# A linear-attention layer: 640 output columns as 512 and 128 on one stationary block, keys one block ahead of values, and the last query norms first

## The chip, the cores and the metric

The kernel runs on one core of a Trainium2 chip. The metric is the device time of one execution in microseconds (us). Engines are named as in the profile: PE (TensorE, with PEld for its weight loads), DVE (VectorE), ACT (ScalarE), POOL (GpSimd) and SP (SyncE, here a queue that issues DMAs).

## The reference, cut to what matters

Four layers run one after the other on 2048 tokens of 640 features: A, B, A, B. Layer A is a recurrent attention with memory in 64 segments and takes most of the time. The change lies in layer B, a linear attention with 32 heads of 20 features:

```
qkv   = layernorm(x) @ wqkv                      # 2048 x 1920
pq,pk = q @ w_phi, k @ w_phi                     # per head, 20 x 20
phi_q = [softmax(pq), softmax(-pq)]              # and phi_k likewise
kv    = sum over tokens of phi_k^T v             # per head, 40 x 20
z     = sum over tokens of phi_k
o     = (phi_q @ kv) / (phi_q . z + 1e-6)
x     = x + o @ wo                               # wo is 640 x 640
```

## The kernel before

Layer B works on 16 blocks of 128 tokens, four blocks to a group, and has two stages with all of `kv` between them.

**First stage, groups 0 to 3.** For each group the rows are normalised and turned with TensorE transposes into `xnT`. `keys_values` (L403) then goes block by block. The keys' 640 columns are two products of 320 columns (`ps_pk`, L410, five matmuls each, one for each 128 input features); ACT takes exp(+) and exp(-) of each half (L413); DVE sums them by head (`sk`, L416) and takes reciprocals (`rk`, L418), which POOL copies into `vr` (L421). The values are again two products of 320 columns (`ps_v`, L425), which DVE scales by `rk` into `vr` (L429). Last come 14 small matmuls that add the block into `kv` (L435); they stay in three PSUM banks over all blocks. After the four blocks, `query_norms` (L451) runs for the group before: two sums over features (`ps_sq`, L457, six matmuls each), a logarithm of each on ACT (L349), exponentials (L342, L343) and DVE steps (L460, L344), and then, for each of the six head groups, one matmul `ps_e` (L465) and a DVE product (L466). Then `queries` (L440) makes six products of 512 columns (`ps_pq`, L446), whose exponentials ACT writes into `phi` (L449).

**Second stage, groups 0 to 3.** `denominators` (L523) is twelve matmuls `ps_den` (L527) with a stationary block of 64 columns, and then L349, L342, L343 and L344. `attention` (L531) makes, for each of six head groups, two matmuls `ps_num` (L538) and one `ps_e` (L541); ACT copies `ps_e` (L543) and DVE multiplies (L544). `output_rows` (L547) makes, for each of four blocks, two products of 320 columns with `wo` (`ps_wo`, L555), six matmuls each, of which five have 120 rows and the last has 40; DVE adds the residual (L557) and POOL issues the store (L559). In the first layer B the rows are also normalised for the layer A after it: DVE statistics (L222), two small POOL casts, ACT (L236, L237), the subtraction on POOL (L244), the scaling on ACT (L248), and a second store from POOL (L563).

Before the first stage, `multiply` (L1192) makes rows that layer A left over, as products of 512 and 128 columns on one stationary block (L1198 into `kv` banks, L1199 into `ps_post`), four times in a layer.

**PSUM.** There are eight banks: three for `kv`, two in the pool `pt` (`side_bank`, for `ps_post`, `ps_sq`, `ps_den` and both `ps_e`), and three in the pool `ps` (`bank`, for all the rest). A buffer that is taken again waits until the last reader of its former tile is done. A scheduler sets the order of layer B's instructions on each engine when the program is built; each engine then runs its instructions in that order.

Of the kernel before, what the change touches and what calls it, by code (L numbers as in the profile page):

```python
# [8 lines left out]
P = 128  # L9
BF16 = mybir.dt.bfloat16  # L10
F32 = mybir.dt.float32
ACT = mybir.ActivationFunctionType
ALU = mybir.AluOpType
# [18 lines left out]
def bcast_last(ap2, n):  # L32
    d = [list(x) for x in ap2.ap]
    assert len(d) == 2, d
    return ap3(ap2, [d[0], d[1], [0, n]])
# [80 lines left out]
class Kernel:  # L116
# [133 lines left out]
    def layer_B(self, x_dram, at_dram, xout_dram, xnext_dram, li, bp, post):  # L250


        nc, tc, KC, D = self.nc, self.tc, self.KC, self.Dm
        DH, H = self.DhB, self.HB
        HC = 6
        CH = DH * HC
        NC_ = -(-H // HC)
        sizes = [min(CH, D - CH * c) for c in range(NC_)]
        NG, NB = self.NG, self.NB
        HB2 = H // 2  # L260
        W2 = D // 2
        at = 0

        def take(nbytes):
# [5 lines left out]
        wo = self.view(take(NC_ * D * 2), NC_ * D * 2).rearrange("p (c m) -> p c m", m=D)  # L270
# [15 lines left out]
        wqkv = self.view(take(6 * D * KC), 6 * D * KC).rearrange("p (k n) -> p k n", k=KC)  # L286
# [3 lines left out]
        x2 = self.view(take(NB * D * 2), NB * D * 2).rearrange("p (b d) -> p b d", d=D)  # L290
# [2 lines left out]
        assert at <= ARENA - fb  # L293
        phi = self.view(ARENA - fb, fb).rearrange("p (s c t) -> p s c t", s=2, c=NC_)
        with tc.tile_pool(name=f"B{li}_kv", bufs=1, space=bass.MemoryType.PSUM, reuse_waits="tile") as kvp, \
                tc.tile_pool(name=f"B{li}_pt", bufs=2, space=bass.MemoryType.PSUM, reuse_waits="tile") as ptp, \
                tc.tile_pool(name=f"B{li}_ps", bufs=3, space=bass.MemoryType.PSUM, reuse_waits="tile") as pp:
            def bank(name="ps_b", dt=F32):
                return pp.tile([P, 512 if dt == F32 else 1024], dt, name=name, tag="bank")

            def side_bank(name):
                return ptp.tile([P, 512], F32, name=name, tag="side")

            nc.gpsimd.memset(wbd[:], 0.0)
            for i in range(HC):
                n = len(range(i, H, HC))
                nc.gpsimd.dma_start(out=wbd[DH * i:DH * i + DH, 0:n, DH * i:DH * i + DH],
                                    in_=self.B_w_phi[i:H:HC].rearrange("h d f -> d h f"))
# [73 lines left out]
            def fuse(j):  # L382
# [17 lines left out]
                        self.ev.copy(out=wqkv[:, k, D * j + CH * c0:D * j + CH * c0 + n], in_=ps[:, 0:n])  # L400
                nc.gpsimd.dma_start(out=self.fused_d[:, :, D * j:D * j + D], in_=wqkv[:, :, D * j:D * j + D])

            def keys_values(g, xnT):  # L403
                for b in range(4 * g, 4 * g + 4):
                    q = P * (b - 4 * g)
                    ek = eks.next().rearrange("p (s d) -> p s d", s=2)
                    for u in range(2):
                        ps = bank("ps_pk")
                        for k in range(KC):
                            nc.tensor.matmul(ps[:, 0:W2], lhsT=xnT[:, k, q:q + P],  # L410
                                             rhs=wqkv[:, k, D + W2 * u:D + W2 * u + W2], start=(k == 0), stop=(k == KC - 1))
                        for sg in range(2):
                            nc.scalar.activation(out=ek[:, sg, W2 * u:W2 * u + W2], in_=ps[:, 0:W2], func=ACT.Exp,  # L413
                                                 scale=1.0 - 2.0 * sg)
                    sk = bp.tile([P, 2 * H], F32, name="sk", tag="sk")
                    nc.vector.reduce_sum(out=sk[:], in_=ek[:, :, :].rearrange("p s (h f) -> p (s h) f", f=DH), axis=AX.X)  # L416
                    rk = bp.tile([P, 2, H], F32, name="rk", tag="rk")
                    nc.vector.reciprocal(out=rk[:, :, :].rearrange("p s h -> p (s h)"), in_=sk[:])  # L418

                    vr = vrs.next().rearrange("p (s h f) -> p s h f", s=2, h=H)  # L420
                    nc.gpsimd.tensor_copy(out=vr[:, :, :, DH], in_=rk[:])  # L421
                    for u in range(2):
                        ps = bank("ps_v")
                        for k in range(KC):
                            nc.tensor.matmul(ps[:, 0:W2], lhsT=xnT[:, k, q:q + P],  # L425
                                             rhs=wqkv[:, k, 2 * D + W2 * u:2 * D + W2 * u + W2], start=(k == 0),
                                             stop=(k == KC - 1))
                        for sg in range(2):
                            nc.vector.tensor_tensor(out=vr[:, sg, HB2 * u:HB2 * u + HB2, 0:DH],  # L429
                                                    in0=ps[:, 0:W2].rearrange("p (h f) -> p h f", f=DH),  # L430
                                                    in1=bcast_last(rk[:, sg, HB2 * u:HB2 * u + HB2], DH), op=ALU.mult)
                    for sg in range(2):
                        for c in range(NC_):
                            nh = sizes[c] // DH
                            nc.tensor.matmul(kv_out(sg, c), lhsT=ek[:, sg, CH * c:CH * c + sizes[c]],  # L435
                                             rhs=vr[:, sg, HC * c:HC * c + nh, :].rearrange("p h f -> p (h f)"),
                                             start=(b == 0 and (NC_ * sg + c) % 4 == 0), stop=(b == NB - 1),
                                             skip_group_check=True)

            def queries(g, xnT):  # L440
                tk = slice(512 * g, 512 * g + 512)
# [50 lines left out]
            waiting = None  # L492
            for g in range(NG):
                if g == 0:
                    xnT = first_xnT
                elif g == 1:
                    with tc.issue_after(turned.ins):
                        xnT = norm_T(g)
                else:
                    xnT = norm_T(g)  # L500
# [21 lines left out]
            def denominators(g):  # L522
                tk = slice(512 * g, 512 * g + 512)  # L523
                ps = side_bank("ps_den")
                for i in range(2 * NC_):
                    sg, c = i // NC_, i % NC_
                    nc.tensor.matmul(ps[0:64, :], lhsT=zm[0:sizes[c], sg, c, :], rhs=phi[0:sizes[c], sg, c, tk],  # L527
                                     start=(i == 0), stop=(i == 2 * NC_ - 1))
                return split_exp(log_rows(ps), -1.0)

            def attention(g, hl):  # L531
                tk = slice(512 * g, 512 * g + 512)
                oT = oTs.next().rearrange("p (c t) -> p c t", c=NC_)
                for c in range(NC_):
                    mc = sizes[c]
                    pn = bank("ps_num")
                    for sg in range(2):
                        nc.tensor.matmul(pn[0:mc, :], lhsT=kvm[0:mc, sg, c, 0:mc], rhs=phi[0:mc, sg, c, tk], start=(sg == 0),  # L538
                                         stop=(sg == 1))
                    pe = side_bank("ps_e")  # L540
                    nc.tensor.matmul(pe[0:mc, :], lhsT=expc[0:64, c, 0:mc], rhs=hl, start=True, stop=True)  # L541
                    rx = rxs.next()
                    nc.scalar.activation(out=rx[0:mc, :], in_=pe[0:mc, :], func=ACT.Copy)  # L543
                    nc.vector.tensor_tensor(out=oT[0:mc, c, :], in0=pn[0:mc, :], in1=rx[0:mc, :], op=ALU.mult)  # L544
                return oT

            def output_rows(g, oT):  # L547
                for b in range(4 * g, 4 * g + 4):
                    q = P * (b - 4 * g)
                    rows = slice(b * P, (b + 1) * P)  # L550
                    ob = obs.next()
                    for u in range(2):
                        ps = bank("ps_wo")
                        for c in range(NC_):
                            nc.tensor.matmul(ps[:, 0:W2], lhsT=oT[0:sizes[c], c, q:q + P],  # L555
                                             rhs=wo[0:sizes[c], c, W2 * u:W2 * u + W2], start=(c == 0), stop=(c == NC_ - 1))
                        nc.vector.tensor_tensor(out=ob[:, W2 * u:W2 * u + W2], in0=ps[:, 0:W2], in1=x2[:, b, W2 * u:W2 * u + W2],  # L557
                                                op=ALU.add)
                    nc.gpsimd.dma_start(out=xout_dram[rows, :], in_=ob[:])  # L559
                    if xnext_dram is not None:  # L560
                        xn = xns.next()
                        self.ln_rows(bp, ob, xn, centre=nc.gpsimd, scale=nc.scalar)
                        nc.gpsimd.dma_start(out=xnext_dram[rows, :], in_=xn[:])  # L563

            hl = denominators(0)
            for g in range(NG):
                oT = attention(g, hl)
                if g + 1 < NG:
                    hl = denominators(g + 1)
                if g == 0:  # L570
                    query_norms(waiting)
                output_rows(g, oT)

    def build_A_consts(self):
# [667 lines left out]
```

## Time and profile before

| | us |
|---|---|
| median of 3 runs | 3689.81 (3688.88 to 3700.95) |
| the profiled execution's own time | 3680.76 |
| its span | 3678.8 |
| first layer B, first stage (from the first `ps_pk` to the first `ps_den`) | 1631 to 1753.6 |
| first layer B, second stage, to layer A's first `ps_pre` | 1753.6 to 1863.3 |
| second layer B, first stage | 3462.9 to 3587.5 |
| second layer B, second stage, to the end of `ps_wo` | 3587.5 to 3669.2 |

All places are us from the span's start. PE is the engine with the most busy time. Its clock, as the profile has it, is full nearly everywhere in layer A, and at one half for parts of layer B's second stage.

### The profile page before, as it was taken

The numbers are of one execution on the slowest core, as the hardware profiler recorded it, in microseconds if no ns is written. First come the engines' busy times: TensorE is split into PE (matmuls) and PEld (weight loads), VectorE is DVE, ScalarE is ACT, GpSimd is POOL, SyncE is SP. The second block draws the span as 40 slices with busy tenths as digits, with TensorE's granted clock in tenths as the row PEclk, the third lists the DMA queues.
The fourth block names the chain that finished last, engine by engine and source line by source line (L and its number), as shares of the span: only waits on it lengthen the run. The fifth ranks groups of instructions, "written<-read, shape, count | busy, mean of one in ns | idle before, by whom it ended". The sixth has DMA issues, their size and how long they took to land.

```text
span 3678.8 us, 168780 instructions
## 1 busy us (share of the span) xinstructions
PE 3527.4 (96%) x70978; PEld 2301.1 (63%) x71271; DVE 2339.3 (64%) x6292; ACT 2044.9 (56%) x5233; POOL 1653.2 (45%) x4309
## 2 busy tenths in 40 slices
PE   9999999999999999999999899999999999999998
PEld 7766666666666666655367666666666666666553
DVE  5566666666666666556433566666666666666464
ACT  3356666666666656546332566666666666666462
POOL 3445555555555555430342455555555555555300
PEclk9999999999999999989799999999999999999998
DMA  8988888888888878840377887888888888888500
GB/s 296 342 296 293 277 279 292 285 277 294 283 274 291 290 266 289 304 140 1 135 255 203 292 286 273 292 290 279 295 283 278 289 288 274 289 293 299 155 1 29
DMA packets 531731, 933.33 MB, mean 254 GB/s; under 512 B 141066, under 2 KB 298394, under 8 KB 530970
## 3 DMA queue, kind: packets, MB, share of 16 engines
q1 hardware_dynamic: 428794, 818.87, 63.6%
q0 software_dynamic: 68512, 90.42, 8.3%
q10 hardware_dynamic: 33664, 13.24, 1.4%
q8 instruction: 557, 9.13, 1.0%
q14 instruction: 204, 1.67, 0.1%
HBM read 852.43 MB, written 73.73 MB: 252 GB/s over the span
## 4 chain that ended last, share of the span: by engine, by line
PE 37%; DMA 6%; DVE 4%; ACT 3%; issue 3%; PEld 2%; POOL 1%; SPq 0%; POOLq 0%; ACTq 0%; DVEq 0%
PE ps_qk L948 10%; PE ps_w L1024 4%; PE ps_v L948 4%; PE ps_o L998 2%; PE ps_s L990 2%; DMA arena<-wo_rows 2%; PE ps_pq L446 1%; PE ps_s L1056 1%; PEld L839 1%; DVE hT L904 1%; PE ps_s L985 1%; DMA kqb<-arena 1%; PE ps_idle L1031 1%; DMA arena<-in_A_Wv_dram 1%; PE ps_pk L410 1%
## 5 line engine op out<-in xcount | busy, mean ns | idle before, releaser
L948 PEld LDWEIGHTS <-hT 128*32 128x32 bf16 x30720 | 738.5, 96 | 433.5 <-DVE hT L1168 29.3
L948 PE MATMUL ps_qk<-arena,hT 128*32 128x384 bf16 x20480 | 996.9, 327 | 12.7 <-DMA arena<-in_A_Wk_dram 3.3
L958 ACT ACTIVATE raw<-ps_qk 128x384 bf16<-128x384 f32 x1024 | 503.1, 491 | 379.1 <-PE ps_s L1056 243.8
L1024 PE MATMUL ps_w<-arena,OT 128*32 128x160 bf16 x24576 | 540.9, 234 | 27.5 <-issue 14.9
L931 POOL DMA_DIRECT2D Vp<-vb x512 | 258.8, 505 | 653.9 <-PE ps_o L998 450.6
L948 PE MATMUL ps_v<-arena,hT 128*32 128x384 bf16 x10240 | 537.4, 330 | 5.6 <-DMA arena<-in_A_Wv_dram 5.5
L1024 PEld LDWEIGHTS <-OT 128*32 128x32 bf16 x24576 | 434.9, 97 | 120.3 <-issue 41.7
L963 DVE STREAM_TRANSPOSE KT<-raw 128x384 bf16<-128x384 bf16 x512 | 296.0, 578 | 196.6 <-ACT raw L958 192.6
L966 DVE STREAM_TRANSPOSE QT<-raw 128x256 bf16<-128x256 bf16 x512 | 227.9, 445 | 238.8 <-ACT raw L958 196.1
L919 POOL DMA_DIRECT2D kqb<-kqb x512 | 291.1, 569 | 174.6 <-POOL KT L927 147.9
L979 DVE CAST Vp<-ps_v 64x384 bf16<-64x384 f32 x512 | 286.0, 559 | 95.4 <-ACT Vp L977 80.5
L1017 POOL DMA_DIRECT2D otb<-otb x512 | 282.8, 552 | 110.1 <-DVE otb L1013 96.3
L977 ACT ACTIVATE Vp<-ps_v 64x384 bf16<-64x384 f32 x512 | 246.3, 481 | 150.7 <-PE ps_v L948 113.2
L1004 DVE CAST OT<-ps_o 128x192 bf16<-128x192 f32 x512 | 183.2, 358 | 214.8 <-PE ps_o L998 196.6
L1063 DVE TENSOR_TENSOR E<-E,ps_s 80x320 bf16<-80x320 bf16 x512 | 247.6, 484 | 73.7 <-ACT ps_s L1062 69.7
L1042 ACT ACTIVATE E<-ps_s 80x320 bf16<-80x320 f32 x512 | 221.9, 433 | 124.2 <-PE ps_s L990 95.7
L998 PEld LDWEIGHTS <-Vp 80*128 80x128 bf16 x4096 | 183.7, 99 | 159.4 <-issue 124.6
L998 PE MATMUL ps_o<-E,Vp 80*128 80x80 bf16 x4096 | 234.5, 202 | 24.4 <-DMA Vp<-vb 5.0
L990 PE MATMUL ps_s<-QT,KT 128*80 128x80 bf16 (+1 forms) x3072 | 233.6, 213 | 21.5 <-DVE KT L963 13.2
L1003 ACT ACTIVATE OT<-ps_o 128x192 bf16<-128x192 f32 x512 | 167.8, 328 | 147.6 <-PE ps_o L998 147.3
L912 ACT ACTIVATE Vp<-ps_w 32x160 bf16<-32x160 f32 x512 | 150.7, 294 | 167.4 <-DVE wt L1167 152.5
L990 PEld LDWEIGHTS <-KT 128*80 128x80 bf16 x3072 | 195.0, 119 | 70.7 <-issue 60.9
(157 smaller groups left out, 5329.9 us busy)
## 6 DMA issues: line engine op xcount, KB each, us to landing
arena<-wo_rows SPq DMA_DIRECT2D x792, 320.0 KB, 6.8
arena<-in_A_Wq_dram SPq DMA_DIRECT2D x427, 384.0 KB, 4.7
arena<-in_A_Wv_dram SPq DMA_DIRECT2D x427, 384.0 KB, 6.3
arena<-in_A_Wk_dram SPq DMA_DIRECT2D x768, 192.0 KB, 4.7
kqb<-kqb POOLq DMA_DIRECT2D x512, 48.0 KB, 5.1
arena<-in_A_Wk_dram SPq DMA_DIRECT2D x43, 384.0 KB, 7.1
vb<-arena POOLq DMA_DIRECT2D x128, 112.0 KB, 6.0
Vp<-vb POOLq DMA_DIRECT2D x512, 28.0 KB, 4.8
```

Of the source, the lines that this page charges most:

```text
L919: nc.gpsimd.dma_start(out=kqb[:], in_=self.kqb_d[s, :, r, :])
L931: nc.gpsimd.dma_start(out=Vs[n % 2][64:80, :], in_=self.vb_d[s, r].rearrange("g t f -> (g t) f"))
L948: nc.tensor.matmul(o[32 * g:32 * g + 32, 0:384], lhsT=hT[:, b, :], rhs=rhs, start=(i == 0), stop=(i == KC - 1), tile_position=(0, 32 * g), ...
L958: nc.scalar.activation(out=raw[:], in_=ps[:, 0:384], func=ACT.Copy)
L963: nc.vector.transpose(out=KT[:, :, 0:64], in_=raw[:, :].rearrange("p (c j) -> p c j", j=64))
L977: nc.scalar.activation(out=o, in_=i, func=ACT.Copy)
L979: nc.vector.tensor_copy(out=o, in_=i)
L990: nc.tensor.matmul(S[0:80, c0:c0 + 80 * (q1 - q0)], lhsT=KT[:, 3 * x + i, :], rhs=QT[:, x, q0:q1, :], start=False, stop=(x == 1 and i == 2 ...
L998: nc.tensor.matmul(O[x][:, 80 * i:80 * i + 80], lhsT=Vs[n % 2][0:80, 448 * x + k:448 * x + k + 128], rhs=E[0:80, 160 * x + 80 * e:160 * x ...
L1017: nc.gpsimd.dma_start(out=self.otb_d[s, :, 96 * r:96 * r + 96], in_=otb[:, :, :].rearrange("p c t -> p (c t)"))
L1024: nc.tensor.matmul(W[32 * g:32 * g + 32, 0:160], lhsT=OT[:, c, q:q + 32], rhs=w[:, 640 * i + 160 * g:640 * i + 160 * g + 160], start=(firs ...
L1063: nc.vector.tensor_tensor(out=E[0:80, 0:320], in0=E[0:80, 0:320], in1=rc, op=ALU.mult)
```

## The change

Where a product of 640 columns was made as 320 and 320, one after the other, `pair` now makes it as 512 and 128 (500 and 140 for the values, at the edge of a head) into two banks, the two matmuls of a step side by side on the same stationary block. In `keys_values` the keys of a block come before the values of the block before it. The pool `pt` has one buffer in place of two, and `ps` has four in place of three; attention's `ps_e` moves from `pt` to `ps`. The query norms of the last group come ahead of all denominators, where they stood after the first group's attention and the second group's denominators.

```diff
-                tc.tile_pool(name=f"B{li}_pt", bufs=2, space=bass.MemoryType.PSUM, reuse_waits="tile") as ptp, \
-                tc.tile_pool(name=f"B{li}_ps", bufs=3, space=bass.MemoryType.PSUM, reuse_waits="tile") as pp:
+                tc.tile_pool(name=f"B{li}_pt", bufs=1, space=bass.MemoryType.PSUM, reuse_waits="tile") as ptp, \
+                tc.tile_pool(name=f"B{li}_ps", bufs=4, space=bass.MemoryType.PSUM, reuse_waits="tile") as pp:
...
+            def pair(name, split, n, lhsT, rhs):
+                ps = [bank(name) for _ in range(2)]
+                for k in range(n):
+                    for i, (lo, hi) in enumerate(((0, split), (split, D))):
+                        nc.tensor.matmul(ps[i][:, 0:hi - lo], lhsT=lhsT(k), rhs=rhs(k, lo, hi), start=(k == 0), stop=(k == n - 1))
+                return (ps[0], 0, split), (ps[1], split, D)
...
             def keys_values(g, xnT):
-                for b in range(4 * g, 4 * g + 4):
+                VS = DH * (512 // DH)
...
+                def keys(b):
                     ek = eks.next().rearrange("p (s d) -> p s d", s=2)
-                    for u in range(2):
-                        ps = bank("ps_pk")
-                        for k in range(KC):
-                            nc.tensor.matmul(ps[:, 0:W2], lhsT=xnT[:, k, q:q + P],
-                                             rhs=wqkv[:, k, D + W2 * u:D + W2 * u + W2], start=(k == 0), stop=(k == KC - 1))
+                    for ps, lo, hi in pair("ps_pk", 512, KC, tokens(b), lambda k, lo, hi: wqkv[:, k, D + lo:D + hi]):
                         for sg in range(2):
...
+                            nc.scalar.activation(out=ek[:, sg, lo:hi], in_=ps[:, 0:hi - lo], func=ACT.Exp, scale=1.0 - 2.0 * sg)
...
+                    return ek, rk
+
+                def values(b, ek, rk):
...
+                    for ps, lo, hi in pair("ps_v", VS, KC, tokens(b), lambda k, lo, hi: wqkv[:, k, 2 * D + lo:2 * D + hi]):
+                        h = slice(lo // DH, hi // DH)
                         for sg in range(2):
...
+                before = None
+                for b in range(4 * g, 4 * g + 4):
+                    now = (b, *keys(b))
+                    if before is not None:
+                        values(*before)
+                    before = now
+                values(*before)
...
-                    pe = side_bank("ps_e")
+                    pe = bank("ps_e")
                     nc.tensor.matmul(pe[0:mc, :], lhsT=expc[0:64, c, 0:mc], rhs=hl, start=True, stop=True)
...
-                    for u in range(2):
-                        ps = bank("ps_wo")
...
+                    for ps, lo, hi in pair("ps_wo", 512, NC_, lambda c: oT[0:sizes[c], c, q:q + P],
+                                           lambda c, lo, hi: wo[0:sizes[c], c, lo:hi]):
+                        nc.vector.tensor_tensor(out=ob[:, lo:hi], in0=ps[:, 0:hi - lo], in1=x2[:, b, lo:hi], op=ALU.add)
...
+            query_norms(waiting)
             hl = denominators(0)
             for g in range(NG):
                 oT = attention(g, hl)
                 if g + 1 < NG:
                     hl = denominators(g + 1)
-                if g == 0:
-                    query_norms(waiting)
                 output_rows(g, oT)
```

## The prediction

> **What bounds the kernel now.** I read the busy times first, then stretches of layer B, then PE's waits, then its timeline. All times in us.
>
> ```profile
> PE 3527.4 (96%) x70978; PEld 2301.1 (63%) x71271; DVE 2339.3 (64%) x6292; ACT 2044.9 (56%) x5233; POOL 1653.2 (45%) x4309
> ```
>
> PE is busy nearly everywhere, but the change touches only the two layers B, some 430 us of the span. By stretch (length, busy time by engine, granted clock, DMA share):
>
> ```profile
> 1691.20:1722.90 31.70, 29.59 (x198) 17.96 (x198) 20.58 (x37) 20.23 (x43) 2.50 (x5) 1.00 0.00 1
> 1753.00:1857.00 104.00, 95.43 (x333) 34.71 (x331) 54.00 (x137) 40.29 (x83) 45.64 (x69) 0.74 0.38 126
> 3590.00:3630.00 40.00, 37.19 (x127) 13.70 (x127) 18.48 (x30) 12.96 (x22) 2.22 (x4) 0.79 0.05 17
> ```
>
> The first is one group of the first stage: PE leads, DVE and ACT have room. The second and third are the second stage of the first layer B and the first half of that of the second: PE looks busy, at a clock of 0.74 and 0.79. It is stretched work, not more of it. What PE waits for (total, times, longest), first layer's first stage, then second layer's:
>
> ```profile
> PE ps_pk L410 <- ACT arena L413: 4.0, 5, 1.1
> PE ps_pq L446 <- ACT arena L449: 1.6, 3, 0.6
> PE kv L435 <- DVE arena L429: 1.0, 2, 0.6
> ...
> PE ps_pk L410 <- ACT arena L413: 5.7, 7, 1.1
> ...
> PE kv L435 <- POOL arena L421: 1.7, 1, 1.7
> ```
>
> The waits of both lists that bear on the change are 9.7 (`ps_pk`), 3.2 (`ps_pq`), 3.7 (`kv`, with small rows), 0.4 (`ps_v`). `ps_pk` waits for a bank: of three, two hold values until DVE has scaled them. The timeline of PE shows what a product costs:
>
> ```profile
> 1556.22 0.38 PE L1198 MATMUL kv<-arena 128*128 128x512 bf16 x1
> 1556.43 0.22 PE L1199 MATMUL ps_post<-arena 128*128 128x128 bf16 x1
> 1556.49 0.38 PE L1198 MATMUL kv<-arena 128*128 128x512 bf16 x1
> ...
> 1760.73 0.59 PE L541 MATMUL ps_e<-arena 64*120 64x512 bf16 x2 [1.93 <-DVE arena L344]
> ...
> 1772.53 5.74 PE L457 MATMUL ps_sq<-arena 120*64 120x512 bf16 x12
> 1778.20 4.63 PE L555 MATMUL ps_wo<-arena 120*128 120x320 bf16 x24
> ...
> 3464.26 1.52 PE L425 MATMUL ps_v<-arena 128*128 128x320 bf16 x10
> 3465.62 0.84 PE L410 MATMUL ps_pk<-arena 128*128 128x320 bf16 x5
> ...
> 3644.29 3.12 PE L527 MATMUL ps_den<-arena 120*64 120x512 bf16 x12
> 3647.34 8.26 PE L555 MATMUL ps_wo<-arena 120*128 120x320 bf16 x48
> 3655.54 0.64 PE L538 MATMUL ps_num<-arena 120*120 120x512 bf16 x2
> ```
>
> A pair of 512 and 128 takes 0.27 (1556.22 to 1556.49). Ten products of 320 take 1.36, two of them 0.272. **The shapes alone buy PE nothing.** The 48 of `ps_wo` take 8.20, not 48 x 0.136 = 6.5: at each change between 120 and 40 rows the next matmul starts about 0.10 late. And twelve `ps_sq` take 5.67 at half clock, twelve `ps_den` 3.05 at full clock.
>
> **What the Trainium skill says.** "TensorE: Matmul & The Clock Gate", Back-to-back issue gap: a warm matmul takes N/2.4 + 2.5 ns, 136 ns for 320 columns; the trace agrees (0.136). Same page, Step-by-step: a weight load is pulled ahead of running matmuls when row groups don't conflict or it goes to the background buffer; the 0.10 at each change of rows fits a load that wasn't. Same page, Part 1: the clock falls to one half after an idle window of about 3.4 us; the half-clock stretches here follow sparse work, but `ps_sq` ran 5.67 us without a gap at half clock, so when it recovers I can't say. "Perfetto Trace Analysis", Optimization Strategy: a gap that repeats can mean too few buffers; the `ps_pk` wait repeats, three times 0.85 in the first group of the second layer.
>
> **The change part by part.**
>
> (1) *Keys ahead, four banks, first stage.* ACT's work stays: 4 x 0.435 = 1.74 a block before, 2 x 0.59 + 2 x 0.27 = 1.73 after (L449 and L1202 have these shapes). DVE's too: 0.484 at 320 columns and 0.69 at 512 (L544) give 0.67 + 0.29 for 500 and 140, against 2 x 0.484. What goes is the waiting: with keys of b+1 between, `rk` of b is ready when its values come, so their banks come free at once, and `kv` finds `vr` done. I walked one group by banks. PE's work in it is 80 key and value products x 0.136 = 10.9, 56 `kv` x 0.084 (ten run in 0.84) = 4.7, 30 `ps_pq` and 18 `ps_sq` and `ps_e` x 0.216 = 10.4, 20 transposes x 0.067 = 1.3, and some ten changes of rows or columns at 0.1: 28.3. With the waits that are left it takes about 30 of the 31.7, limited late by the run `sk` 1.48, `rk` 0.55, four scalings 1.93 on DVE, 4.0 a block. Removed: 9.7 + 3.7 + 0.4, and half of 3.2 for the fourth bank: 15.4. The half kept is ACT's own, 1.19 a product against PE's 1.08. POOL's copy L421 moves behind the next block's keys, with nothing that waits behind it. No DMA moves on SP; on POOL, stores and casts only swap neighbours.
>
> (2) *One side bank, first stage.* The second `ps_sq` set now waits for the first's logarithm (0.59); in the built order key products stand between, cost nothing unless ACT is late. A `ps_e` round is 0.45 to the DVE product, 0.68, and 0.06 back: 1.19. The built order puts some four `ps_pq` (0.86) between, so 0.1 is open, five times; with late DVE 0.5 a group, six groups: +3. Bounds: 0, and 5.8 a group (six rounds uncovered, 35 in all). (1) and (2): -12.4.
>
> (3) *Last query norms first.* `ps_den` shares the one side bank, so it waits for all of them. From the last exponential of group 3: first sums 0.5, logarithm 0.6, second sums 1.5, then logarithm 0.65, subtraction 0.74, two exponentials 1.3, subtraction 0.7: 6.0. Six rounds of 1.19: 13.1. `ps_den` 2.6, logarithm 0.65, nine of the next twelve 2.0, by when `split_exp` of group 0 is done: 18.7. Attention of group 0, some 5.8: 24.5 to the first `ps_wo`. Cold: 0.2 more in each round, 1.3 in the second sums, 0.21 in each of 21 `ps_den`: 31.4. Before: 1754.9 to 1778.2 = 23.3, and 3588.7 to 3609.0 = 20.3. So +5 in both layers together if warm, +19 if cold; I take +12. Their old place beside `ps_wo` hid them; the stall of 1.93 on L344, twice, goes.
>
> (4) *Second stage from the first `ps_wo`, second layer.* Before 3609.0 to 3669.2 = 60.2. After: a block of `wo` is 6 x 0.272 plus two row changes of 0.1, 1.83, instead of 2.05; four make 7.3. Attention with four shared banks has two head groups under way, each 2.3 long (`ps_e` 0.67, ACT 0.59, DVE 0.69, hand-overs): 7.0 for six, and the twelve `ps_den` between (30 matmuls, 6.5) hide in it. 4 x 7.3 + 3 x 7.0 = 50.2, and 1.7 for a cold start: 51.9, **-8.3** (-10 to -3).
>
> (5) *The same, first layer, to layer A's first product.* Before 1778.2 to 1863.3 = 85.1. Here POOL works on every block: 1.88 (L244), stores 0.57 and 0.56, casts 0.38, 3.4. In the built order ACT's `ps_e` copies alternate with its L248, which waits for POOL, so a group can't end before POOL's fourth block: 4.0 to the first statistics, 4 x 3.4, 0.83 + 0.59 + 0.69: 19.7. Three of these and the last `wo` with its tail, 15.3 as before: 74.4, **-10.7** (0 if the clock stays as low as now; -24 if POOL doesn't gate).
>
> (6) `ps_post` in one bank: seven 512-column matmuls (1.5) stand ahead in the built order to cover its copy (0.27, or behind a 1.35 copy): +1 for six seams, 0 to 3. Pools and ring buffers in SBUF stay.
>
> Sum: -12.4 + 12 - 8.3 - 10.7 + 1 = **-18.4**. Against the profiled execution's 3680.8 that is 3662; it ran 9 below the median of the runs, 3689.8, from which I forecast **3671**.
>
> **The rivals.** *Slower: the one side bank.* Both starts of (3) run cold (+19), the low clock carries on and eats (4) and (5), and half of each group's rounds stay uncovered (3 a group, six groups, +18) against -15.4: about +22, 3712. Single rounds in series speak for it; the key and query products between them in the built order speak against. It decides once open side-bank waits pass the 15 us that the keys give back. *No change: layer A's start is set elsewhere.* (5) gives nothing, since the rows' statistics and POOL set the end, and DVE in the first stage eats half of (1): -12.4 + 7 + 12 - 8 + 1, about 0: 3689. For it: the chain that ended last runs through L244 and L248 there. Against: PE's own clock loss. *Larger gain: the clock stays full.* Fewer holes, so (3) is +5, (5) -20, (4) -10: -37, 3653. *Not what it says:* one stationary block for two products would save loads, but the built program has as many weight loads as before (71,108); so no gain is counted there.
>
> **How the numbers follow.** A measurement can tell 0.3%, 11 us. Main case 0.50 (3659 to 3680), larger gain 0.17, no change 0.18, slower 0.15. Faster by over 0.3%: 0.48 + 0.17 = 0.65; within: 0.02 + 0.18 = 0.20; slower 0.15. The range, 3646 to 3698, takes in the bounds of (3) and (5) together and leaves out the far ends of the larger gain and of the slower case.
>
> **What would show it.** Right: `ps_pk` on L413 nearly gone from the waits, groups of 29 to 30; one gap of some 10 around the last `ps_sq`; `ps_wo` blocks of 1.83; groups of 14 to 15 in the second layer's second stage and near 20 in the first's. Wrong: `ps_sq` or `ps_e` high among PE's waits in the first stage; `ps_den` at half clock in both layers; groups of the first layer's second stage still at 23.

## The result, and the profile after

The changed kernel takes 3698.76 us (median of 22 runs, 3667.2 to 3720.97) against 3689.76 for the kernel before (22 runs beside it): a ratio of 1.0019, 95% interval 1.0000 to 1.0037. So there is no gain, and by the interval a loss of 0 to 14 us. The forecast was 3671, with a range of 3646 to 3698.

The profiled execution of the changed kernel is the slowest of its 22 runs: 3720.97 us, span 3718.9, 40.1 more than the span before. Stage by stage the two spans compare as follows, both layers B added up (places of first and last matmuls in the trace; the half-clock time is from the clock record):

| stretch, us | before | after | difference | step of the prediction |
|---|---|---|---|---|
| first stage, first `ps_pk` to last `ps_pq` | 122.5 + 124.4 | 116.6 + 119.6 | -10.7 | (1), (2): -12.4 |
| last `ps_pq` to first `ps_wo` | 24.8 + 21.7 | 43.2 + 42.0 | **+38.7** | (3): +12 |
| second layer, first to last `ps_wo` | 59.7 | 54.2 | -5.5 | (4): -8.3 |
| first layer, first `ps_wo` to first `ps_pre` | 85.1 | 83.8 | -1.3 | (5): -10.7 |
| first `ps_post` to first `ps_pk` | 74.8 + 59.0 | 74.7 + 58.8 | -0.3 | (6): +1 |
| layers B in all | 571.9 | 592.9 | +21.0 | -18.4 |
| layers A (first to last `ps_qk`) | 1370.8 + 1364.2 | 1376.0 + 1381.3 | +22.3 | not counted |
| half-clock time in the whole span | 148.6 | 203.4 | +54.8 | not summed |

The change touches no instruction of layers A. Over all kernels below the first of them took 1370 to 1386 in the profiled executions and the second 1364 to 1382 (one apart, e4_warm), so a single profile is worth some ten us there. The stretches in layer B are what is compared below, and medians of runs for the whole. Keep in mind that these "after" stretches come from the slowest execution, 22 us above the median one, so they probably show the loss larger than it is in most runs; no other execution of this kernel was profiled.

The page's line of busy times:

```profile
PE 3544.2 (95%) x70946; PEld 2285.9 (61%) x71271; DVE 2336.0 (63%) x6292; ACT 2043.7 (55%) x5233; POOL 1655.3 (45%) x4309
```

PE is 16.8 us busier than before on the same products, while all other engines are the same within 4 but PEld, 15 lower. The half-clock time is 54.8 us longer, so a slower clock is the likely reason. Here are the stretches (length, busy time by engine with instruction counts, granted clock, DMA share, GB/s): one group of the first stage, then the walk to the first `ps_wo` and what is behind it, in the first and in the second layer B.

```profile
1689.90:1719.90 30.00, 29.87 (x195) 15.94 (x196) 20.23 (x38) 19.55 (x42) 2.02 (x5) 1.00 0.01 1
1750.30:1793.50 43.20, 31.99 (x66) 8.98 (x64) 12.86 (x29) 9.55 (x16) 0.00 (x0) 0.55 0.40 146
1793.50:1871.20 77.70, 70.75 (x269) 25.20 (x269) 43.22 (x111) 29.42 (x65) 45.09 (x69) 0.73 0.26 83
3612.40:3654.40 42.00, 30.80 (x66) 8.73 (x64) 12.86 (x29) 9.54 (x16) 0.00 (x0) 0.57 0.00 0
3654.40:3708.60 54.20, 54.20 (x269) 21.56 (x269) 28.67 (x52) 15.68 (x26) 8.06 (x15) 0.96 0.12 43
```

The first line is the gain: a group takes 30.0 in place of 31.7, and PE hardly waits in it. The second and fourth are the loss, beside the same two walks in the kernel before:

```profile
1753.40:1778.20 24.80, 22.29 (x56) 6.78 (x55) 6.06 (x17) 9.11 (x16) 0.00 (x0) 0.68 0.69 257
3587.30:3609.00 21.70, 19.30 (x57) 6.23 (x55) 6.09 (x16) 8.99 (x16) 0.00 (x0) 0.76 0.00 1
```

PE now waits for 11.2 us in each walk, where it waited for 2.5 and 2.4, and it is busy for 32.0 and 30.8, where it was for 22.3 and 19.3, at a clock of 0.55 and 0.57 in place of 0.68 and 0.76. So there are two losses on top of each other, some 9 us more of waiting and some 10 us more of busy time in each layer, the latter at a lower clock and with about ten more matmuls.

PE's waits (total, times, longest): the first stage of the second layer first, then the walk of the first layer:

```profile
PE kv L439 <- POOL arena L429: 2.4, 1, 2.4
PE ps_v L406 <- ACT arena L420: 2.4, 3, 1.1
...
PE ps_e L477 <- DVE arena L478: 4.9, 7, 0.8
PE ps_e L477 <- DVE arena L342: 3.4, 1, 3.4
PE ps_den L539 <- DVE arena L478: 0.8, 1, 0.8
PE ps_sq L469 <- DVE arena L478: 0.8, 1, 0.8
```

The `ps_pk` waits on ACT, 4.0 and 5.7 before, are gone. The sums of the norms, `ps_e` at L477, now wait for the DVE product L478 that reads the sum before them: that is the one side bank. The list of the second layer's walk is the same. PE's timeline of the first layer's walk (start, length, line, tile, shape, count, in brackets the idle time before it and its releaser):

```profile
1752.98 0.37 PE L477 MATMUL ps_e<-arena 64*40 64x512 bf16 x1 [0.78 <-DVE arena L478]
1754.13 2.73 PE L469 MATMUL ps_sq<-arena 120*64 120x512 bf16 x6 [0.77 <-DVE arena L478]
1757.53 2.85 PE L469 MATMUL ps_sq<-arena 120*64 120x512 bf16 x6 [0.68 <-ACT arena L347]
1763.83 0.58 PE L477 MATMUL ps_e<-arena 64*120 64x512 bf16 x1 [3.44 <-DVE arena L342]
1765.19 0.58 PE L477 MATMUL ps_e<-arena 64*120 64x512 bf16 x1 [0.78 <-DVE arena L478]
...
1771.98 5.69 PE L539 MATMUL ps_den<-arena 120*64 120x512 bf16 x12 [0.77 <-DVE arena L478]
1778.35 4.27 PE L539 MATMUL ps_den<-arena 120*64 120x512 bf16 x9 [0.68 <-ACT arena L347]
1782.55 0.68 PE L553 MATMUL ps_e<-arena 64*120 64x512 bf16 x1
...
1793.51 3.81 PE L406 MATMUL ps_wo<-arena 120*128 120x512 bf16 x12
```

Read it as one queue for one bank. The last spread sum of **group 2** holds it until 1754; then come two sums of group 3 (L469), a chain of logarithms and exponentials with PE idle for 3.44, six spread sums 1.36 apart, and only then the `ps_den` of group 0, which needs nothing of the norms of group 3. From 1754.3 the clock record shows one half for 44.4 us, past the end of the walk, and in the second layer from 3618.0 for 41.0.

### The profile page after: what moved, and what is told of

Read it like the earlier page. It is cut to its first block, busy times and chain, and to the rows that moved or that the text cites. A ratio compares the mean times of both kernels' runs of the same rounds, so it can differ in the third digit from the quotient of the medians.

```text
span 3718.9 us, 168711 instructions
## 1 busy us (share of the span) xinstructions
PE 3544.2 (95%) x70946; PEld 2285.9 (61%) x71271; DVE 2336.0 (63%) x6292; ACT 2043.7 (55%) x5233; POOL 1655.3 (45%) x4309
## 4 chain that ended last, share of the span: by engine, by line
PE 59%; DMA 15%; DVE 7%; issue 7%; ACT 5%; POOL 2%; PEld 2%; SPq 1%; POOLq 0%; DVEq 0%; ACTq 0%
PE ps_qk L955 19%; PE ps_w L1031 8%; PE ps_v L955 8%; DMA arena<-wo_rows 6%; PE ps_o L1005 4%; PE ps_s L997 4%; DMA arena<-in_A_Wv_dram 3%; PE ps_s L1063 2%; DVE hT L911 2%; PE ps_s L992 2%; PE ps_idle L1038 2%; DMA kqb<-arena 2%; ACT raw L965 2%; DVE E L1070 1%; PEld L846 1%
## 5 line engine op out<-in xcount | busy, mean ns | idle before, releaser
L955 PEld LDWEIGHTS <-hT 128*32 128x32 bf16 x30720 | 739.9, 96 | 437.5 <-DVE hT L1175 27.9
L931 POOL COPY QT<-kqb 128x64 bf16<-128x64 bf16 x512 | 126.4, 247 | 253.5 <-PE ps_s L997 245.5
```

The lines of the kernel that those rows point to most:

```text
L955: nc.tensor.matmul(o[32 * g:32 * g + 32, 0:384], lhsT=hT[:, b, :], rhs=rhs, start=(i == 0), stop=(i == KC - 1), tile_position=(0, 32 * g), ...
```

## The experiments

All ratios are to the kernel before, run beside each on the same chip. "Walk" is the stretch from the last `ps_pq` to the first `ps_wo`, first and second layer, with its half-clock time in brackets; "stage" is the first stage.

| kernel | median us (runs) | ratio, 95% | stage | walk |
|---|---|---|---|---|
| the changed kernel | 3698.76 (22) | 1.0000 to 1.0037 | 116.6, 119.6 | 43.2 (39.2), 42.0 (36.5) |
| e1_norms_back | 3663.74 (8) | 0.991 to 0.996 | 115.2, 119.6 | 17.4 (0), 17.4 (0) |
| e2_norms_first_alone | 3693.99 (22) | 1.0007 to 1.0031 | 122.7, 126.5 | 30.2 (20.5), 29.6 (17.1) |
| e3_two_side | 3698.56 (22) | 1.0005 to 1.0033 | 120.8, 124.5 | 29.6 (13.7), 26.7 (6.8) |
| e4_warm | 3725.46 (6) | 1.0069 to 1.0121 | 116.1, 121.2 | 42.4 (20.5), 37.6 (6.8) |
| e4b_warm_aligned | 3694.37 (22) | 0.9999 to 1.0022 | 115.4, 118.3 | 38.2 (10.2), 39.8 (13.7) |
| e5_halves | 3671.22 (12) | 0.9939 to 0.9975 | 111.3, 117.4 | 19.6 (3.4), 22.3 (10.2) |
| e6_no_ahead | 3672.46 (20) | 0.9943 to 0.9972 | 115.4, 121.0 | 19.6 (3.4), 22.2 (10.2) |
| e7_dve_centre | 3659.71 (6) | 0.9904 to 0.9956 | 114.5, 119.6 | 17.4 (0), 26.5 (21.2) |
| e8_norm_banks | 3680.95 (12) | 0.9965 to 0.9988 | 127.8, 130.6 | 20.4 (0), 20.4 (0) |
| e9_last_norms_banks | 3685.01 (14) | 0.9973 to 1.0010 | 114.5, 119.6 | 27.9 (10.2), 37.6 (32.3) |
| e10_both | 3675.04 (21) | 0.9946 to 0.9973 | 114.5, 118.2 | 31.0 (17.1), 27.9 (10.2) |
| e11_den_first | 3674.58 (14) | 0.9956 to 0.9986 | 114.5, 115.9 | 20.7 (10.2), 22.1 (13.7) |

**e1_norms_back**: the whole change, with the norms back in their old place.

```diff
-            query_norms(waiting)
             hl = denominators(0)
...
+                if g == 0:
+                    query_norms(waiting)
                 output_rows(g, oT)
```

> The change with one edit taken back: the last query norms stand again after the first group's attention and the second group's denominators. Theory A (the norms ahead of everything, in series on one side bank, let TensorE's clock fall to one half for some 40 us in each layer B, and that costs what the first stage gains): from the last ps_pq to the first ps_wo some 25 us instead of 43 and 42, half-clock stretches there of 10 to 20 us instead of 44 and 41, time 20 to 38 us below the changed kernel, so 3662 to 3679 and below the kernel before. Rival B (the one side bank and the pairs cost the time wherever the norms stand): the gap moves to later ps_wo rows, and the time stays at 3690 to 3700. Rival C (layer A's chain varies and the difference is there): within 5 us of the changed kernel.

Measured: 3663.74, below both kernels; the intervals of its ratio and of the changed kernel's lie far apart. The walk is 17.4 in both layers, all at full clock:

```profile
1746.30:1763.70 17.40, 14.97 (x54) 5.12 (x53) 7.94 (x22) 8.15 (x14) 0.00 (x0) 1.00 0.92 333
3568.80:3586.20 17.40, 14.97 (x53) 5.08 (x51) 7.94 (x22) 8.09 (x15) 0.00 (x0) 1.00 0.00 1
```

Its timeline at the same place as above:

```profile
1748.94 0.37 PE L477 MATMUL ps_e<-arena 64*40 64x512 bf16 x1 [0.78 <-DVE arena L478]
1750.08 3.10 PE L539 MATMUL ps_den<-arena 120*64 120x512 bf16 x12 [0.77 <-DVE arena L478]
1753.85 2.33 PE L539 MATMUL ps_den<-arena 120*64 120x512 bf16 x9 [0.68 <-ACT arena L347]
```

The first `ps_den` follows the last spread sum of group 2 at once, and the same twelve and nine matmuls take 3.10 and 2.33 in place of 5.69 and 4.27. So moving these norms alone costs the changed kernel 35 us of median (3698.76 - 3663.74; 31 by the two ratios, 1.0019 and 0.9935), and all else in the change together gains 26 over the kernel before. The move takes away both the waiting and the half clock, so this run doesn't part the two.

**e2_norms_first_alone**: the kernel before, with only this move (the reverse of the diff of e1_norms_back).

> The kernel before with one edit: the last query norms first. Two side banks and three others, products of 320 columns. Theory A: most of the cost of the whole change without its gain: last ps_pq to first ps_wo 35 to 42 us instead of 25 and 22, a half-clock stretch of 27 us or more in each layer B, time 3705 to 3725. If the one side bank is what makes the place costly (rival B), two banks hide half of each round, the gap is 25 to 30 us and the time 3690 to 3700.

Measured: 3693.99, a walk of 30.2 and 29.6. With two side banks the same move costs about 4 us by the medians (3 to 11 by the interval), not 35. Its six spread sums stand between 1766.29 and the first `ps_den` at 1770.00, 3.7 us, where the changed kernel's take 8.15 (1763.83 to 1771.98). Place and bank have to be taken together: the place alone is cheap here, and the one side bank alone, in e1_norms_back, costs nothing that shows.

**e3_two_side**: the changed kernel with the pools of before, two side banks and three common ones.

```diff
-                tc.tile_pool(name=f"B{li}_pt", bufs=1, ...
-                tc.tile_pool(name=f"B{li}_ps", bufs=4, ...
+                tc.tile_pool(name=f"B{li}_pt", bufs=2, ...
+                tc.tile_pool(name=f"B{li}_ps", bufs=3, ...
```

> The changed kernel with two side banks and three others; norms first, pairs and keys ahead kept. Theory A: the six rounds get shorter (0.7 to 0.9 us instead of 1.36, some 4 us a layer), but the clock still falls, so the gap is 35 us or more; the first stage loses part of its 5 us a layer since two pairs no longer fit: time 3690 to 3710. Rival B (one side bank decides): gap below 28 us, time below 3680.

Measured: 3698.56, equal to the changed kernel. The walk is 14 and 15 shorter, -29 in all, and the first stage is back at 120.8 and 124.5, +9. That the medians are equal nevertheless is most likely the choice of executions: the two profiled ones lie 24.0 apart, and of that 23.8 is that the changed kernel was profiled 22.2 above its median and this one 1.6 below. So the walk's 43.2 and 42.0 may well not be typical of the changed kernel. The interval also overlaps that of e2_norms_first_alone: with the norms first, the trade of a side bank for a fourth common one gives nothing. What it does show is that keys ahead and the shapes, with three banks, leave the first stage within 2 us of before.

**e4_warm**: the changed kernel with 36 added products of 128x512 beside the norms of each layer B, whose sums nobody reads.

```diff
+            def warm(n, t):
+                for _ in range(n):
+                    nc.tensor.matmul(kv_ps[2][:, 0:512], lhsT=t[:, 0:P], rhs=t, start=True, stop=True, skip_group_check=True)
...
-            query_norms(waiting)
+            query_norms(waiting, True)
```

> The changed kernel with 36 matmuls of 128x512 added in each layer B while the last query norms run in series, into a kv bank that nothing reads again: same results, same waits, more TensorE work. Theory A: the clock stays full or nearly so through norms, denominators and the first attention; rounds of 1.2 instead of 1.36, 21 ps_den in 5 to 6 us instead of 10, last ps_pq to first ps_wo 28 to 32 us instead of 43 and 42; time 18 to 28 us below the changed kernel, 3671 to 3681. If the waits alone cost the time and the clock only shows them (rival D), the added work changes nothing or adds up to 8 us a layer: 3699 to 3715.

Measured: the half-clock time in the walks fell to 20.5 and 6.8, and layers B to 576.9, 16 below the changed kernel in these two executions, yet the time rose to 3725.46. The second layer A took 1396.6 instead of 1381.3. PE's waits in it:

```profile
PE ps_s L1005 <- issue: 19.3, 28, 2.0
PE ps_v L963 <- issue: 5.5, 14, 1.1
```

Neither the changed kernel nor e1_norms_back or e3_two_side has this `ps_s` wait in its list for this layer's chain. "Issue" is waiting for nothing that the profile shows. Layer A begins with a number of idle weight loads (79 in the second), which suggested that the place of its instructions in PE's stream matters, and 36 products with a weight load each, 72 instructions, had been added ahead of it.

**e4b_warm_aligned**: the same, with 72 of these idle weight loads taken out.

```diff
-FILL = {0: 86, 2: 79}
+FILL = {0: 86, 2: 7}
```

> The kernel of e4_warm (the changed kernel with 36 added products of 128x512 beside the serial norms in each linear layer, written into a PSUM bank that the linear layer has no more use for) with 72 fewer of the idle weight loads that the second recurrent layer begins with (7 in place of 79), so that this layer's instructions stand where they stand in the changed kernel. Theory A (the clock gained in the linear layers was given back because the 72 added instructions shift the second recurrent layer's instructions against the engine's fetching): that layer's chain returns from 1396.6 us to 1371-1382, the linear layers stay at 570-580, the time is 3675-3690 us. Rival D (the recurrent layer is slower for another reason, or the warm start spends clock that is withheld later): the chain stays over 1390 and the time at 3712-3730.

Measured: the second layer A is back at 1366.8 and the `ps_s` wait has left the list; the median fell by 31 to 3694.37. The loads that were taken out can't have cost that much themselves: in e4_warm all 79 take 1.03 us together. So the count of instructions ahead did cost e4_warm its gain. That it is instruction fetching is argued, not shown. The time is still 4 above the upper end of theory A, and the interval overlaps the changed kernel's: keeping TensorE busy during a serial walk buys little here. A likely reason is that the added products stand in PE's queue themselves (36 x 0.216 = 7.8 us a layer, an estimate at full clock).

**e5_halves**: e1_norms_back with two halves of 320, one after the other.

```diff
-                for k in range(n):
-                    for i, (lo, hi) in enumerate(((0, split), (split, D))):
+                for i, (lo, hi) in enumerate(((0, D // 2), (D // 2, D))):
+                    for k in range(n):
```

> The changed kernel with the last query norms in their old place (e1_norms_back, 3663.7 us) and the products of 640 columns again as two halves of 320, one half after the other; four banks, one side bank and keys ahead stay. Theory A (512 and 128 side by side buys next to nothing by itself; only the output product, whose row counts alternate, loses some 0.2 us for each of 16 blocks in two layers, and in the first layer GpSimd hides it): 3662-3674 us, first stages within 3 us of 115.2 and 119.6. Rival E (the shapes carry the gain of the first stage): first stages over 120 and 124, time over 3678.

Measured: 3671.22, first stages of 111.3 and 117.4, not longer than with the shapes. The second layer's output stretch is 58.9 against 55.9, about the 0.22 a block by which the prediction priced the row changes (16 blocks, 3.5). The interval of the whole overlaps that of e1_norms_back. The shapes don't carry the gain of the first stage.

**e6_no_ahead**: e1_norms_back with each block's values directly behind its keys.

```diff
-                before = None
                 for b in range(4 * g, 4 * g + 4):
-                    now = (b, *keys(b))
-                    if before is not None:
-                        values(*before)
-                    before = now
-                values(*before)
+                    values(b, *keys(b))
```

> The changed kernel with the last query norms in their old place (e1_norms_back) and with the values of a block directly behind its own keys; four banks, one side bank and the 512 and 128 shapes stay. Theory G (four common banks give the gain of the first stage, and keys ahead is worth little beside them, since a scheduler may place the next keys early anyway): first stages 115-119 and 119-122 us, time 3660-3672. Theory H (keys ahead gives it): first stages 120-124 and 122-127, time 3672-3684.

Measured: 3672.46 with first stages of 115.4 and 121.0, within 1.4 of e1_norms_back: the stages say theory G, and the median is half a us above G's range, in H's by as little. With e3_two_side and e5_halves this leaves the fourth common bank as what gives the first stage its gain; it is found by taking away, since the kernel before with only a fourth common bank was not run. A likely reason is that the scheduler orders the instructions by itself, so that here the order of lines was worth little once a bank was free.

**e7_dve_centre**: e1_norms_back, with the centring of the output rows on DVE.

```diff
-                        self.ln_rows(bp, ob, xn, centre=nc.gpsimd, scale=nc.scalar)
+                        self.ln_rows(bp, ob, xn, scale=nc.scalar)
```

> The changed kernel with the last query norms in their old place (e1_norms_back, 3663.7 us), and the centring in output_rows on VectorE in place of GpSimd (where it takes 1.88 us of each block's chain). It exists in the first linear layer alone. Theory A (GpSimd sets the pace of the first layer's second stage, about 4 us for a block of 128 tokens, so a faster TensorE there buys nothing): the stretch from the first ps_wo to the last falls from 75.6 us to 58-68, the time to 3646-3658 us. Rival F (the pace is set by TensorE's and VectorE's own queues, and GpSimd's waits are only handed down): the stretch is 73-80, since VectorE has more to do, the time 3661-3670.

Measured: 3659.71, the lowest median, though not told apart from e1_norms_back. The stretch from the first `ps_wo` to the last in the first layer, of e1_norms_back and then of this kernel, with the two largest waits of ACT in e1_norms_back's stretch (to layer A's first product):

```profile
1763.70:1839.30 75.60, 66.35 (x283) 24.45 (x282) 47.09 (x118) 30.71 (x67) 44.88 (x69) 0.84 0.28 92
```

```profile
1765.60:1830.40 64.80, 61.07 (x283) 23.59 (x282) 51.59 (x131) 31.49 (x67) 21.09 (x57) 0.92 0.33 108
```

```profile
ACT ln_lv L236 <- POOL ln_mvr L229: 23.3, 11, 6.3
ACT arena L248 <- POOL arena L244: 11.0, 9, 1.9
```

75.6 became 64.8 with 24 us of work taken off POOL and 4.5 put on DVE. POOL was busy for only 44.9 of the 75.6, so it is not POOL's load alone that sets the pace. What is left is the round DVE, POOL, ACT, POOL, ACT that each block makes before the next products find their copies done; that reading is argued from ACT's waits. The clock rose with it, from 0.84 to 0.92, and PE's busy time fell by 5.3, so part of the 10.8 may be clock. In this execution the walk of the second layer, where the edit changes nothing, was 9 us longer (26.5, with 21.2 at half clock), which hides most of the gain in its time.

**e8_norm_banks**: the changed kernel, norms first, with the norms' spread sums in the common banks.

```diff
-                    pe = side_bank("ps_e")
+                    pe = bank("ps_e")
```

> The changed kernel with one name altered: the six spread sums ps_e of query_norms are taken from the four common banks, where the change leaves them in the single side bank; the last query norms stay ahead of the first denominators. Theory A (the single side bank draws the serial walk out: each spread sum waits for the multiplication that reads the one before): the stretch from the last ps_pq to the first ps_wo falls from 43.2 and 42.0 us to 28-33, about what the kernel before shows with only the norms put first (30.2 and 29.6), the time to 3672-3686 us. Theory B (with the norms first the place alone costs what was lost, whatever bank the sums are in): both stretches stay over 38 us and the time at 3692-3704.

Measured: 3680.95, a walk of 20.4 in both layers at full clock, shorter than either theory said, with the norms still first. In this kernel's order the twelve `ps_den` of group 0 go ahead of the spread sums, since they no longer stand behind them for a bank. The loss moved to the first stage, where a group takes 34 to 35 in place of 30, with 20.5 and 23.9 us of the two stages at half clock, where the changed kernel has 4.5 and 6.8. PE's longest waits in the second layer's:

```profile
PE ps_e L477 <- DVE arena L342: 5.6, 3, 2.0
```

The likely reading is that the six sums, taken together from the common banks, hold up what they used to slip between.

**e9_last_norms_banks**: the same for the last group only.

```diff
-                    pe = side_bank("ps_e")
+                    pe = side_bank("ps_e") if g + 1 < NG else bank("ps_e")
```

> The changed kernel with the spread sums ps_e of the last group's query norms alone in the common banks; those of groups 0 to 2 stay in the single side bank, so the first stage is the changed kernel's. Theory A (the cost of norms first is that their six spread sums stand ahead of the first denominators in the single side bank; with that undone the place costs little): last ps_pq to first ps_wo 19-23 us in both layers in place of 43.2 and 42.0, first stages 114-121, time 3655-3672 us. Theory B (the place costs by itself, through sparse work and a half clock): that stretch stays over 28 us and the time at 3680 or more.

Measured: the first stage keeps its gain, but the walk is 27.9 and 37.6 and the time 3685.01. Theory A missed both; theory B's time is met and its stretch in one layer of two. The pair of layers tells why. From the first `ps_den` to the first `ps_wo`, first layer and second:

```profile
1751.89:1769.87 17.98, 17.98 (x56) 5.78 (x55) 9.40 (x15) 7.94 (x14) 0.00 (x0) 0.86 0.50 193
3587.40:3615.44 28.04, 28.04 (x55) 7.38 (x55) 9.98 (x15) 8.28 (x14) 0.00 (x0) 0.50 0.00 0
```

Both run the same instructions in the same order, and PE waits for nothing in either. Both begin at half clock. In the first layer the clock was full again from 1757.0, 5 us into the stretch, and it took 17.98; in the second the half clock was granted throughout, and it took 28.04. The bank accounts for the order; the clock alone accounts for these 10 us.

**e10_both**: e9_last_norms_banks with the diff of e7_dve_centre.

> The kernel of e9_last_norms_banks with the centring in output_rows on VectorE in place of GpSimd (first linear layer alone). If GpSimd paces the first layer's second stage here too, the stretch from the first ps_wo to the last falls by 6-12 us to 58-66 and the time by as much below e9_last_norms_banks, to 3646-3664 us. If not, both stay within 3 us of it.

Measured: the output stretch fell from 73.4 to 60.6 and the time by 10 to 3675.04, outside the range given, since its base came out higher too. The gain on the round through POOL is there on either base.

**e11_den_first**: the changed kernel with two lines swapped.

```diff
-            query_norms(waiting)
             hl = denominators(0)
+            query_norms(waiting)
```

> The changed kernel with two lines swapped: the first denominators are asked for ahead of the last query norms, in place of behind them; both still use the single side bank, in the order of the lines. Theory A (what costs is that the denominators, and all attention behind them, stand in the side bank's line behind two sums and six spread sums of the norms): in the built order the twelve ps_den, the two sums and the attention of group 0 now go ahead of the norms' six spread sums, which lie between the output products; last ps_pq to first ps_wo 16-22 us in both layers in place of 43.2 and 42.0, at full clock for most of it, time 3655-3672 us. Theory B (norms ahead of the first attention cost by themselves, or the one side bank does wherever they stand): that stretch stays over 28, or what it loses comes back in the groups that follow, and the time is 3680 or more.

Measured: the walk is 20.7 and 22.1, as theory A has it (22.1 by a tenth outside), but 10 to 14 us of each are at half clock, and the time is 3674.58, between the two theories. So of the 35 us, the swap of two lines gives back 24 (by the ratios, 18 of 31): the first denominators' place in the side bank's line is the greater part of the loss. Why this kernel's clock fell and that of e1_norms_back didn't, when both enter the walk with the same twelve `ps_den` after the same waits, stays open.

## Why the prediction was wrong

**The failed step is (3), "last query norms first": +12 forecast, +38.7 measured.** The runs say the same without the profile: with the norms at their old place all other steps together gained 26, where their forecasts add up to 30, and the norms' move cost 35 where +12 was forecast. The mechanism, "`ps_den` shares the one side bank, so it waits for all of them", is what happened; the size was off. Even its cold case, "31.4 if cold", counted from the last exponential, falls about 10 short of a walk of 43.2 from the last `ps_pq`, 1.5 us earlier. In the first layer two terms make up these 10, on top of the cold case, and the third error is the choice of a value:

- It began with the sums of group 3 already under way ("first sums 0.5"). In the built order the last spread sums of group 2 still held the side bank, two rounds with nothing to cover them, so the first sums started at 1754.13, took 2.73 and ended at 1756.9, 5.0 us after the last exponential (1751.8): +4.5.
- Attention of group 0 was 5.8 at full clock in both cases. It ran at half clock, from 1782.55 to 1793.51, 11.0: +5.2.
- The half clock was weighed as one of two cases, and the value taken, +12, lay midway between +5 and +19. In the profiled execution it held for 39.2 of the 43.2 and 36.5 of the 42.0. Rounds, sums and the chain between were sized well for the cold case: rounds of 1.36 against 1.19 + 0.2, the chain 3.44 against 0.65 + 0.74 + 1.3 + 0.7 = 3.39. (Its terms up to the end of `split_exp` add up to 18.4 where 18.7 stands; nothing hangs on these 0.3.)

This execution was the slowest, so the +38.7 is at the upper end. The half clock explains part of that: 203 us in it against 170 in the median run. The clock has a price that the prediction never summed over the whole kernel. Over the 22 runs of the changed kernel, time rises by 0.41 us for each us at half clock (half-clock time worked out as 2 x (1 - mean clock) x span; correlation 0.86). The Trainium skill, "TensorE: Matmul & The Clock Gate", Terms, puts the penalty at throttled time x (1 - K/N), a half at a half clock; the runs agree, a little below. The medians are 170 us at half clock for the changed kernel and 106 for e1_norms_back; 64 x 0.41 = 26 of the 35 us between them, an estimate from a fit. The walks of the two traces show 17.6 us more of waiting as well, which together with 26 is over 35, so the split between clock and waits is rough and stays open.

**Step (5) failed too, -10.7 forecast, -1.3 measured.** Groups of the first layer's second stage stayed at 23.6, 23.1 and 21.3 us (starts of `ps_wo`), where POOL's 3.4 a block was to give 19.7. POOL's duration was right, and the clock there stayed low, 0.73, for which the prediction had named 0 as its bound. But the clock is not all of it: in e1_norms_back, with 0.84 over most of the stretch, it still took 81.8 where 74.4 was forecast. Taking the subtraction off POOL brought it to 69.6 in e7_dve_centre, so the block's whole round, not POOL's 3.4 alone, is the likelier pace. This is one of the wrong signs that the prediction named ("still at 23").

**Right, or nearly.** (1) and (2): -10.7 measured against -12.4, groups of 29.8 and 30.0 in both layers (the first ones 28.7 and 31.7, by the starts of `ps_pk`) against "29 to 30", `ps_pk` on ACT gone from the waits, and no side-bank wait of weight in the first stage. But the credit to keys ahead was wrong, so the number came right by another road: the fourth bank gave it. "The shapes alone buy PE nothing" held apart from `wo`, whose four blocks take 7.3 in place of 8.2, as forecast. (4): -5.5 against -8.3; (6): nothing.

**The rivals.** "Slower: the one side bank" named the right bank and both cold starts, but looked for half its loss in the first stage, where there was none. Only its first term, both starts cold, came true. "Larger gain: the clock stays full" is near what e1_norms_back does, 3653 against 3663.74, but that kernel has the norms at their old place. No step and no rival had what that run also shows: with the norms left there, the walk itself falls from 24.8 and 21.7 to 17.4 and 17.4.

## What to carry to other kernels

In this program a PSUM pool of one buffer is a queue in the order of the source's lines: before moving work ahead, list what stands behind it in that pool, needed or not. When a serial stretch is formed, price it at half clock too, through to the next dense stage and into that stage's start. And test the parts of a combined change one by one: here one part cost 35 us, more than the 26 that the others together had gained.

## What the runs showed of the hardware that was not expected

- The half clock can outlast dense work. In e9_last_norms_banks PE ran from 3587.40 to 3615.44 with no wait that the profile shows and stayed at half clock for all 28 us. The Trainium skill, "TensorE: Matmul & The Clock Gate", Part 1: The HAM clock gate, has the clock back after some 3.4 us of sustained work. The measurement decides: here it took over eight times as long. Much of that work has a stationary block of 64 columns or rows of 64 (`ps_den`, `ps_e`); whether that is the reason was not tried. It can't be the whole reason, since in the first layer the clock came back 5 us into the same work.
- The same instructions, begun at half clock, left it after 5 us in one layer and not within 28 us in the other, and ended 10 us apart. Single profiles of this kernel can't rank two orders that differ by less.
- 72 instructions more ahead of a layer made it longer, 1396.6 against 1381.3 in the changed kernel, with `ps_s` waits of 19.3 us put down to "issue". Taking as many idle weight loads out removed these waits: 1366.8, and 31 us less by the medians. Waits that the profile shows don't make up all of it, and the cause stays open.
